# Seven products of quarters for every eight in the second mixture, with its weights streamed

## The chip, the core and the metric

The kernel runs on one core of one Trainium2 chip. The metric is the device time of one execution, in microseconds (us). Before the change it was 1636.01 us, the median of three runs (1632.27 to 1636.53). The execution that the profiler recorded took 1633.56 us.

TensorE (PE) multiplies matrices and writes the sums to eight banks of PSUM. VectorE (DVE) and ScalarE (ACT) read these banks and work on SBUF, GpSimd (POOL) works on SBUF alone, and SyncE (SP) issues most of the DMA transfers. Each of them takes its own instructions in order and waits at semaphores for the others.

## The reference

An attention without a softmax over scores gives 4608 tokens of 512 features. They go through a gated mixture, and then through a second one, which the change is about:

```python
def _moe_ref(x, w_gate, w_val, w_out, rms_g):
    rms = np.sqrt(np.mean(x * x, axis=-1, keepdims=True) + 1e-06)
    xn = x / rms * rms_g
    g = xn @ w_gate                      # 512 x 1536
    silu = g * (1.0 / (1.0 + np.exp(-g)))
    val = xn @ w_val                     # 512 x 1536
    return (silu * val @ w_out)          # 1536 x 512

def _moe2_ref(x, w1, w2, w3, w_out):
    h = np.maximum(np.maximum(x @ w1, x @ w2), x @ w3)   # each 512 x 768
    return (h @ w_out)                                   # 768 x 512
```

The weights arrive as 64-bit floats, which the kernel reads as pairs of 32-bit words and joins to 32-bit floats.

## The kernel before

The tokens are cut into nine groups of 512. Every matrix product is made of `128x512` matmuls in the type `fp32r`. As that type drops low bits, each operand is split into a high part `hi` (a cast, on ACT) and the rest `lo` (a subtraction, on DVE or POOL), and each block of a product takes three matmuls: hi by hi, hi by lo, lo by hi (`product_in`, L423; `three`, L430).

**The first mixture** fills the first two thirds of the time: 9 groups by 12 feature blocks `f`, in `iteration` (L494). One iteration has twelve matmuls for the gate into bank `G`, twelve for the value into bank `V`, and twelve of `out1` (L468) for the block before. Around them ACT takes the tanh of the gate (L541), DVE makes the product `t` and its `lo` part (L542, L553, L560), and the attention of the next group is computed in pieces. Three buffers with the tag `y` serve the squares of the norm (L329), the Newton steps, the results that leave for DRAM (L437) and the weights of the second mixture.

**The class `Ahead`** (L155) prepares those weights during groups 1 to 7, one step in each iteration: join the words of a piece of `128x512` into a `y` buffer (ACT, three instructions on DVE); split it into the piece's own load buffer `st` (ACT, POOL); write both parts to DRAM from `st` and load the next piece. There are 24 pieces: six feature blocks by three matrices, and six of the out matrix. In group 8, `fetch` (L196) brings everything back into SBUF, two transfers of 768 KB in each of eight iterations, to stay there.

**The second mixture** (L608) goes through the groups one by one, and through six feature blocks `f` in each: three products of twelve matmuls into the banks `G`, `V` and `a0`; a copy (L622) and two maxima (L624) that leave the largest in `t`; the split of `t` into `hh` and `hl`; and `out2` (L598), twelve matmuls for the block before. The inputs of the next group are loaded and split meanwhile (L480, L491).

The order of the instructions on each engine is set when the program is built, by a list scheduler that starts from the order of the code; a tile with a tag waits until its buffer is free. So the order that was written is kept on PE, while instructions of other engines and DMA issues move past each other.

Of the kernel before, what the change touches and what calls it, by code (L numbers as in the profile page):

```python
# [28 lines left out]

VW = 672  # L30
# [7 lines left out]
def attention_moe_moe(ctx: ExitStack, tc: tile.TileContext, q, k, kt, v, w1, rms_g, w2, w2_out, out):  # L38

# [42 lines left out]
    w2_dram = [dram.tile([P, 2, 3, N], F32, tag=f"w2_{s}", name=f"w2_dram_{s}") for s in range(NF2 + 2)]  # L82
# [72 lines left out]
    class Ahead:  # L155
# [4 lines left out]
        def __init__(self, pieces):  # L160
            self.pieces = pieces
            self.st, self.y = {}, {}
            self.loaded = 0

        def load(self):
            i = self.loaded
            if i < len(self.pieces):
                slot, j, src = self.pieces[i]
                self.st[i] = two.tile([P, 2 * N], I32, tag="st", name=f"st2_{slot}_{j}")
                nc.sync.dma_start(self.st[i], src.bitcast(I32))  # L170
# [272 lines left out]
    second = Ahead(  # L443
# [24 lines left out]
    def out1(g, f):  # L468
# [227 lines left out]
```

## Time and profile before

| what | us or share |
|---|---|
| median of three runs | 1636.01 |
| profiled execution, its own time | 1633.56 |
| its span, first to last instruction | 1631.8 |
| busy: PE, DVE, ACT, POOL | 97%, 45%, 30%, 12% |
| groups 1 to 7 of the first mixture, roughly 165 to 975 us | PE busy 809.68 of 810 |
| second mixture, from about 1038 us | PE busy without a gap to 1627.6 |

A matmul's row shows 0.39 us, but matmuls are pipelined, so what one costs is the distance between two starts. The granted clock of PE is 1.00 (the level of 2.4 GHz) from about 165 us to the end. Bytes: 130.15 MB in all, 80 GB/s on average.

### The profile page before, as it was taken

To read this page: it belongs to the slowest core of one execution; us is meant where nothing else is said; L and a number is where in the kernel's file an instruction comes from. 1 tells how busy PE (TensorE), PEld (TensorE's weight loads), DVE (VectorE), ACT (ScalarE), POOL (GpSimd) and SP (SyncE) were. 2 spreads that over 40 slices of the span, in tenths; PEclk is the share of its full clock that TensorE was granted. 3 is DMA by queue.
4 is the path that set the end of the run, shared out by engine and by line. 5 is a ranking of instruction groups with operands and counts; after the bars stand their busy time and mean duration, and the time that the engine had idled before them with its cause. 6 is when DMAs were issued, how large, how long until landed. Compare 5 with 4: busy or idle time off the path is not lost.

```text
span 1631.8 us, 18095 instructions
## 1 busy us (share of the span) xinstructions
PE 1585.3 (97%) x7190; PEld 1309.6 (80%) x7190; DVE 732.2 (45%) x1210; ACT 481.5 (30%) x806; POOL 199.4 (12%) x221
## 2 busy tenths in 40 slices
PE   5788999999999999999999999999999999999998
PEld 4576788888888888888888888888888888888887
DVE  6999655655646555565452422322222212222211
ACT  4554333433334333343332321211212112112111
POOL 4455121121221111212100000000000000000000
PEclk8899999999999999999999999999999999999999
DMA  7652241331423313313111045201101001010000
GB/s 257 255 191 79 92 132 58 116 96 48 138 88 111 113 58 117 107 55 111 55 46 33 6 162 194 78 0 52 52 1 52 26 27 52 1 52 26 1 26 26
DMA packets 72676, 130.15 MB, mean 80 GB/s; under 512 B 6032, under 2 KB 30608, under 8 KB 72592
## 3 DMA queue, kind: packets, MB, share of 16 engines
q1 hardware_dynamic: 62224, 110.12, 20.2%
q10 hardware_dynamic: 10368, 18.88, 3.2%
q8 instruction: 56, 0.92, 0.2%
q14 instruction: 28, 0.23, 0.0%
HBM read 95.42 MB, written 33.55 MB: 79 GB/s over the span
## 4 chain that ended last, share of the span: by engine, by line
PE 91%; DVE 5%; issue 2%; POOL 1%; DMA 1%; ACT 1%; SPq 0%; ACTq 0%; DVEq 0%; POOLq 0%
PE p L428 9%; PE p L427 9%; PE p L426 9%; PE acc L433 8%; PE acc L432 8%; PE acc L431 8%; PE pg L426 6%; PE pg L428 6%; PE pg L427 6%; PE pv L428 5%; PE pv L426 5%; PE pv L427 5%; PE pk L266 2%; DVE y L135 1%; PE pt L286 1%
## 5 line engine op out<-in xcount | busy, mean ns | idle before, releaser
L624 DVE TENSOR_TENSOR t<-t,p 128x512 f32<-128x512 f32 x108 | 74.2, 687 | 402.1 <-PE p L428 402.1
L542 DVE SCALAR_TENSOR_TENSOR t<-t,pg 128x512 f32<-128x512 f32 x106 | 72.7, 686 | 131.8 <-ACT t L541 130.8
L556 ACT CAST hh<-t 128x512 fp32r<-128x512 f32 x108 | 66.9, 619 | 159.4 <-DVE t L553 159.3
L541 ACT ACTIVATE t<-pg 128x512 f32<-128x512 f32 x106 | 63.1, 596 | 153.9 <-PE pg L428 153.9
L553 DVE TENSOR_TENSOR t<-t,pv 128x512 f32<-128x512 f32 x108 | 73.1, 677 | 59.6 <-PE pv L428 58.1
L560 DVE TENSOR_TENSOR hl<-t,hh 128x512 fp32r<-128x512 f32 x97 | 70.7, 729 | 60.5 <-ACT hh L556 59.8
L78 ACT CAST hh<-t 128x512 fp32r<-128x512 f32 x54 | 33.4, 618 | 210.2 <-DVE t L624 210.2
L622 ACT COPY t<-p 128x512 f32<-128x512 f32 x54 | 31.7, 587 | 192.7 <-PE p L428 192.7
L233 POOL TENSOR_TENSOR q<-q,qm 128x512 f32<-128x512 f32 x34 | 38.9, 1143 | 156.0 <-DVE qm L232 145.8
L190 POOL TENSOR_TENSOR st<-y,st 128x512 fp32r<-128x512 f32 x24 | 32.1, 1337 | 211.1 <-ACT st L189 190.2
L79 DVE TENSOR_TENSOR hl<-t,hh 128x512 fp32r<-128x512 f32 x54 | 37.4, 692 | 36.2 <-ACT hh L78 36.2
L242 POOL TENSOR_TENSOR q<-q,qr 128x512 f32<-128x512 f32 x34 | 38.6, 1137 | 61.0 <-DVE qr L241 59.0
L330 POOL TENSOR_TENSOR sacc<-sacc,sq 128x512 f32<-128x512 f32 x24 | 32.9, 1370 | 89.6 <-ACT sq L329 86.0
L266 PE MATMUL pk<-v,k 128*128 128x129 f32 x300 | 41.0, 286 | 1.1 <-DVE kv_raw L276 0.8
L432 PE MATMUL acc<-wl_(3, 1)_8004,hh 128*128 128x512 f32 x108 | 42.1, 389 | 0.0
L431 PE MATMUL acc<-wh_(3, 0)_7953,hh 128*128 128x512 f32 x108 | 42.0, 389 | 0.0
L432 PE MATMUL acc<-wl_(3, 0)_7954,hh 128*128 128x512 f32 x108 | 42.0, 389 | 0.0
L431 PE MATMUL acc<-wh_(3, 1)_8003,hh 128*128 128x512 f32 x108 | 42.0, 389 | 0.0
L433 PE MATMUL acc<-wh_(3, 0)_7953,hl 128*128 128x512 f32 x108 | 42.0, 389 | 0.0
L433 PE MATMUL acc<-wh_(3, 1)_8003,hl 128*128 128x512 f32 x108 | 42.0, 389 | 0.0
L266 PEld LDWEIGHTS pk<-v,k 128*128 128x128 f32 x300 | 37.9, 200 | 1.9 <-ACT qh L296 1.1
L438 ACT ACTIVATE oe<-acc 128x512 f32<-128x512 f32 x36 | 20.6, 597 | 50.2 <-PE acc L433 46.0
(474 smaller groups left out, 4438.9 us busy)
## 6 DMA issues: line engine op xcount, KB each, us to landing
words<-in_w SPq DMA_DIRECT2D x24, 768.0 KB, 7.2
w_dram<-st SPq DMA_DIRECT2D x24, 512.0 KB, 3.1
k<-in_k SPq DMA_DIRECT2D x30, 320.0 KB, 4.2
v<-in_v SPq DMA_DIRECT2D x30, 320.0 KB, 4.4
st<-in_w SPq DMA_DIRECT2D x18, 512.0 KB, 4.2
x<-xe ACTq DMA_DIRECT2D x36, 256.0 KB, 2.5
xraw<-x SPq DMA_DIRECT2D x36, 256.0 KB, 3.3
out<-oe ACTq DMA_DIRECT2D x36, 256.0 KB, 2.0
```

Of the source, the lines that this page charges most:

```text
L266: nc.tensor.matmul(pk[:, 0 : P + 1], k_t[g, p][:, c, :], v_t[g, p][:, c, :], start=(c == 0), stop=(c == 4))
L426: nc.tensor.matmul(pt, hi[:, j, s], xhs[kk], start=(kk == 0), stop=False)
L427: nc.tensor.matmul(pt, hi[:, j, s], xls[kk], start=False, stop=False)
L428: nc.tensor.matmul(pt, lo[:, j, s], xhs[kk], start=False, stop=(kk == 3))
L431: nc.tensor.matmul(pt, ah, bh, start=first, stop=False)
L432: nc.tensor.matmul(pt, ah, bl, start=False, stop=False)
L433: nc.tensor.matmul(pt, al, bh, start=False, stop=last)
L542: nc.vector.scalar_tensor_tensor(t, t, 1.0, pg, op0=ALU.add, op1=ALU.mult)
L553: nc.vector.tensor_mul(t, t, pv)
L556: nc.scalar.copy(hh[g, f], t)
L560: (nc.gpsimd if ahead else nc.vector).tensor_sub(hl[g, f], t, hh[g, f].bitcast(F32))
L624: nc.vector.tensor_max(t, t, pj)
```

## The change

The scheme is Strassen's, in Winograd's form, on 2 by 2 quarters. A *unit* `u` is one of the three matrices for a pair of feature blocks, `fp` and `fp + 3`; its left matrix has quarters of 128 features by 256 inputs, and its right one quarters of 256 inputs by 512 tokens, the tokens of two groups side by side. Instead of eight products of quarters (six matmuls each) there are seven. Four sums of the weights (`S1` to `S4`) are made once, in the preparation; four sums of the inputs (`T1` to `T4`) once for each of the four pairs of groups (`combine`). The seven products of a unit go into four banks `a` to `d` (tags `G`, `V`, `a0`, `a1`), three of them on top of what an earlier product left there, and the sums of the results are made by ACT, DVE and POOL (`unit`, L751). The ninth group is computed with four products of each unit, as before in amount.

Seven quarters of each of nine units, each hi and lo, make 63 pieces, kept in DRAM as 21 chunks of 768 KB; a ring of six buffers (`RING`) brings them in again for every pair, 84 chunks, and twelve more for the ninth group, these in three transfers each. The inputs take 28 planes in the buffers of the first mixture's weights. A step of `Ahead` now has a cost, and an iteration room for two or three of them (`advance`); a quarter that is written to DRAM sits in a `y` buffer until the write has landed. `out2` takes two feature blocks at a time, and at the end of a pair four calls stand together.

```diff
+UNITS = 9
+QUARTERS = 7
+CHUNK = 3
+A11, S2, S1, S3, A12, S4, A22 = range(QUARTERS)
+RING = ("wh0", "wl0", "wh1", "wl1", "wh2", "wl2")
+LATER_H = ("xh0", "xh1", "xh2", "xh3", "xl0", "xl1", "xl2", "xl3", "qh", "ql", "sacc", "kT")
...
-    w2_dram = [dram.tile([P, 2, 3, N], F32, tag=f"w2_{s}", name=f"w2_dram_{s}") for s in range(NF2 + 2)]
+    chunk_dram = [
+        dram.tile([P, CHUNK, 2, N // 2], F32, tag=f"w2_{c}", name=f"w2_dram_{c}")
+        for c in range(UNITS * QUARTERS // CHUNK)
+    ]
+    wo_dram = [dram.tile([P, 2, 3, N], F32, tag=f"wo_{s}", name=f"wo_dram_{s}") for s in range(2)]
...
+            self.steps = []
+            for u in range(UNITS):
+                self.steps += [(self.join, (2 * u,)), (self.join, (2 * u + 1,)), (self.sums, (u,))]
+                self.steps += [(self.quarter, (u, n)) for n in (A11, A12, S3, S4)] + [(self.load, ())]
+                self.steps += [(self.quarter, (u, n)) for n in (A22, S1, S2)] + [(self.load, ())]
+            for i in range(len(self.outs)):
+                self.steps.append((self.join, (2 * UNITS + i,)))
+                self.steps += [(self.half, (i, h)) for h in range(2)] + [(self.load, ())]
...
-        def step(self, n):
-            i, part = divmod(n, 3)
-            if i >= len(self.pieces):
-                return
-            slot, j, _ = self.pieces[i]
-            if part == 0:
-                words = self.st[i].rearrange("p (n t) -> p n t", t=2)
-                low, high = words[:, :, 0], words[:, :, 1]
-                nc.scalar.activation(high.bitcast(F32), high.bitcast(F32), AF.Copy, scale=2.0**-112)
-                self.y[i] = two.tile([P, N], F32, tag="y", name=f"y2_{i}", bufs=3)
-                y = self.y[i].bitcast(I32)
-                nc.vector.tensor_scalar(y, high, 3, None, op0=ALU.logical_shift_left)
-                nc.vector.scalar_tensor_tensor(y, high, -(2**31), y, op0=ALU.bitwise_and, op1=ALU.bitwise_or)
-                nc.vector.scalar_tensor_tensor(y, low, 29, y, op0=ALU.logical_shift_right, op1=ALU.bitwise_or)
-            elif part == 1:
-                st, y = self.st[i].bitcast(F32R), self.y.pop(i)
-                nc.scalar.copy(st[:, 0:N], y)
-                nc.gpsimd.tensor_sub(st[:, N : 2 * N], y, st[:, 0:N].bitcast(F32))
-            else:
-                st = self.st.pop(i).bitcast(F32).rearrange("p (t n) -> p t n", t=2)
-                nc.sync.dma_start(w2_dram[slot][:, :, j, :], st)
-                self.load()
...
+        def sums(self, u):
+            t = self.places(u)
+            nc.vector.tensor_add(t[S1], t["A21"], t[A22])
+            nc.vector.tensor_sub(t[S2], t[S1], t[A11])
+            nc.vector.tensor_sub(t[S4], t[A12], t[S2])
+            nc.vector.tensor_sub(t[S3], t[A11], t["A21"])
+
+        def split(self, src, dst, name):
+            t = two.tile([P, 2, N // 2], F32R, tag="y", name=name, bufs=3)
+            nc.scalar.copy(t[:, 0, :], src)
+            nc.gpsimd.tensor_sub(t[:, 1, :], src, t[:, 0, :].bitcast(F32))
+            nc.sync.dma_start(dst, t.bitcast(F32))
+
+        def quarter(self, u, n):
+            i = QUARTERS * u + n
+            self.split(self.places(u)[n], chunk_dram[i // CHUNK][:, i % CHUNK], f"wq_{u}_{n}")
...
+            room = 3 if 1 <= f <= 8 else 2
+            while self.steps:
+                step, args = self.steps[0]
+                writes = step in (self.quarter, self.half)
+                cost = 0 if step == self.load else 1 if writes else 2
+                if cost > room or writes and f > 9:
+                    return
+                room -= cost
+                self.steps.pop(0)
+                step(*args)
...
+    ring, fetched = {}, [0]
+    wanted = [(p, c, None) for p in range(NPAIR) for c in range(UNITS * QUARTERS // CHUNK)]
+    single = [QUARTERS * u + n for u in range(UNITS) for n in (A11, A12, S1, A22)]
+    wanted += [(NPAIR, c, single[CHUNK * c : CHUNK * c + CHUNK]) for c in range(len(single) // CHUNK)]
+
+    def fetch(count=1):
+        for _ in range(count):
+            i = fetched[0]
+            if i >= len(wanted):
+                return
+            p, c, parts = wanted[i]
+            t = wpool.tile([P, CHUNK, 2, N // 2], F32R, tag=RING[i % len(RING)], name=f"chunk_{p}_{c}")
+            if parts is None:
+                nc.sync.dma_start(t.bitcast(F32), chunk_dram[c])
+            else:
+                for n, part in enumerate(parts):
+                    nc.sync.dma_start(t[:, n].bitcast(F32), chunk_dram[part // CHUNK][:, part % CHUNK])
+            ring[p, c] = t
+            fetched[0] += 1
...
-            second.step(NF1 * (g - 1) + f)
-        if nxt is None and 1 <= f <= NF2 + 2:
-            second.fetch(f - 1)
+            second.advance(f)
+            if g == NG - 2 and f == NF1 - 1:
+                assert not second.steps
+        if nxt is None:
+            if 1 <= f <= 3:
+                fetch(2)
+            if f in (4, 5):
+                for n in range(4 * f - 16, 4 * f - 12):
+                    combine(0, n)
+            if f >= 6:
+                for which in {6: (B11,), 7: (T2,), 8: (T1,), 9: (T3,), 10: (B21, B22), 11: (T4,)}[f]:
+                    split_operand(which)
+            if f == 11:
+                fetch_out(0)
...
-    for g in range(NG):
-        for f in range(NF2):
-            if g + 1 < NG:
-                if f == 0:
-                    second_x(g + 1)
-                if 1 <= f <= 4:
-                    split_second_x(g + 1, f - 1)
-            wkey = (2, f)
-            banks = []
-            for j, tag in enumerate(("G", "V", "a0")):
-                pj = bank(tag, f"p2_{g}_{f}_{j}")
-                product_in(pj, wh[wkey], wl[wkey], j, xh2[g], xl2[g])
-                if j == 0:
-                    t = two.tile([P, N], F32, tag="t", name=f"t2_{g}_{f}")
-                    nc.scalar.copy(t, pj)
-                else:
-                    nc.vector.tensor_max(t, t, pj)
-            hh[g, f] = two.tile([P, N], F32R, tag="hh", name=f"hh2_{g}_{f}")
-            hl[g, f] = two.tile([P, N], F32R, tag="hl", name=f"hl2_{g}_{f}")
-            split(hh[g, f], hl[g, f], t)
...
+    def product2(pt, pr, n, which, first, last):
+        w = ring[pr, n // CHUNK][:, n % CHUNK]
+        for kk in range(2):
+            s = slice(kk * P, (kk + 1) * P)
+            i = 4 * which + 2 * kk
+            opens, ends = first and kk == 0, last and kk == 1
+            three(pt, w[:, 0, s], w[:, 1, s], plane(i), plane(i + 1), opens, ends, not first and pr < NPAIR)
...
+        def largest(dst, x, pt, y):
+            if j == 0:
+                nc.vector.tensor_add(dst, x, pt)
             else:
+                nc.vector.tensor_add(y, x, pt)
+                nc.vector.tensor_max(dst, dst, y)
+
+        product2(a, pr, n + A11, B11, True, True)
+        nc.scalar.copy(s1, a)
+        product2(b, pr, n + S2, T2, True, True)
+        nc.vector.tensor_add(u2, s1, b)
+        product2(c, pr, n + S1, T1, True, True)
+        nc.scalar.copy(s5, c)
+        nc.gpsimd.tensor_add(w, u2, s5)
+        product2(d, pr, n + S3, T3, True, True)
+        largest(t[1, 1], w, d, y0)
+        product2(a, pr, n + A12, B21, False, True)
+        if j == 0:
+            nc.scalar.copy(t[0, 0], a)
+        else:
+            nc.vector.tensor_max(t[0, 0], t[0, 0], a)
+        product2(c, pr, n + S4, B22, False, True)
+        largest(t[0, 1], u2, c, y1)
+        product2(d, pr, n + A22, T4, False, True)
+        largest(t[1, 0], u2, d, y0)
...
+            unit(pr, u, t)
+            consumed(pr, QUARTERS * (u + 1))
+            if j == 2:
+                for row in range(2):
+                    split_h(g, fp + H * row, t[row, 0], False)
+                for row in range(2):
+                    split_h(g + 1, fp + H * row, t[row, 1], True)
+            if pr == 0 and u == 0:
                 out1(NG - 1, NF1 - 1)
-    out2(NG - 1, NF2 - 1)
+                fetch_out(1)
+            if j == 0 and fp > 0:
+                out2(g, ACC, (fp - 1, fp - 1 + H))
+            if u == 1:
+                load_raw(pr + 1)
+            if 3 <= u < 7:
+                for n in range(2 * u - 6, 2 * u - 4) if pr + 1 < NPAIR else range(2) if u == 3 else ():
+                    combine(pr + 1, n)
+        for which in range(7) if pr + 1 < NPAIR else (B11, B21, T1):
+            split_operand(which)
+        out2(g + 1, ("G", "V", "a0", "a1"), (0, H, 1, 1 + H))
+        out2(g, ACC, (2, 2 + H), True)
+        out2(g + 1, None, (2, 2 + H), True)
...
```

**The second mixture on DVE**, where PE's banks are read. Before, one row of two maxima and a subtraction for each feature block (`p2` is the product in PSUM, `t2` the largest so far, `hl2` the low part):

```order
L624 TENSOR_TENSOR t2_0_1_8261<-t2_0_1_8261,p2_0_1_1_8263 128x512
L624 TENSOR_TENSOR t2_0_1_8261<-t2_0_1_8261,p2_0_1_2_8277 128x512
L79 TENSOR_TENSOR hl2_0_1_8292<-t2_0_1_8261,hh2_0_1_8291 128x512
L624 TENSOR_TENSOR t2_0_2_8326<-t2_0_2_8326,p2_0_2_1_8328 128x512
L624 TENSOR_TENSOR t2_0_2_8326<-t2_0_2_8326,p2_0_2_2_8342 128x512
L79 TENSOR_TENSOR hl2_0_2_8357<-t2_0_2_8326,hh2_0_2_8356 128x512
```

Now, the last unit of the first pair (`temps_wh9` holds s1, s5 and u2, `temps_wl9` holds w, y0 and y1; the rows on `x2_` are low parts of the next pair's inputs, from `sums_` and `raw2_`):

```order
L90 TENSOR_TENSOR x2_wl4_8175<-raw2_1_1_8599,x2_wh4_8172 128x512
L772 TENSOR_TENSOR temps_wh9_8452<-temps_wh9_8452,p2_0_8_V_9074 128x512
L90 TENSOR_TENSOR x2_wl4_8175<-sums_b_8071,x2_wl4_8175 128x512
L90 TENSOR_TENSOR x2_wh5_8226<-sums_b_8071,x2_wh5_8226 128x512
L90 TENSOR_TENSOR x2_wl5_8275<-sums_a_8070,x2_wh5_8226 128x512
L766 TENSOR_TENSOR temps_wl9_8453<-temps_wl9_8453,p2_0_8_a1_9076 128x512
L90 TENSOR_TENSOR x2_wl5_8275<-sums_a_8070,x2_wl5_8275 128x512
L767 TENSOR_TENSOR t2_0_2_t_8927<-t2_0_2_t_8927,temps_wl9_8453 128x512
L782 TENSOR_TENSOR t2_0_2_q_8924<-t2_0_2_q_8924,p2_0_8_G_9073 128x512
```

Eight instructions of a unit read the banks and the sums, and in a pair's last unit the subtractions for the next pair's inputs stand between them, ahead of the reads of bank `d` (tag `a1`, L766) and of bank `a` (tag `G`, L782).

**The first mixture on ACT**, between two tanh (L541 before, L651 now) of group 4. Before (`st2` and `y2` belong to `Ahead`):

```order
L541 ACTIVATE t_4_1_4221<-pg_4_1_4208 128x512
L189 CAST st2_4_0_3907<-y2_12_4194 128x512
L189 CAST st2_4_1_4107<-y2_13_4416 128x512
L556 CAST hh_4_1_4238<-t_4_1_4221 128x512
L78 CAST qh_5_0_4265<-pt_5_0_4260 128x512
L78 CAST kvh_5_0_4281<-kv_raw0_99 128x128
L541 ACTIVATE t_4_2_4315<-pg_4_2_4302 128x512
```

Now (`wq` is a quarter's `y` buffer, `st2_12` the next load):

```order
L651 ACTIVATE t_4_1_4351<-pg_4_1_4338 128x512
L226 CAST wq_5_3_4388<-st2_10_3803 128x256
L226 CAST wq_5_5_4392<-st2_10_3803 128x256
L666 CAST hh_4_1_4368<-t_4_1_4351 128x512
L226 CAST wq_5_6_4398<-st2_11_3895 128x256
L226 CAST wq_5_2_4490<-st2_11_3895 128x256
L89 CAST qh_5_0_4407<-pt_5_0_4402 128x512
L226 CAST wq_5_1_4494<-st2_11_3895 128x256
L204 ACTIVATE st2_12_4396<-st2_12_4396 128x512
L89 CAST kvh_5_0_4423<-kv_raw0_114 128x128
L651 ACTIVATE t_4_2_4457<-pg_4_2_4444 128x512
```

Five quarters are cast between the two tanh, out of three `y` buffers, and the scaling of the next load stands ahead of the second tanh too.

**SP's queue at the end of the first pair of the second mixture**. Before, SP had only the next groups' inputs (`xraw2`) to load there:

```order
L202 DMA wl_(3, 1)_8004<-w2_dram_7_85 128x1536
L489 DMA xraw2_1_0_8167<-x2_1_70 128x512
L489 DMA xraw2_1_1_8169<-x2_1_70 128x512
L489 DMA xraw2_1_2_8171<-x2_1_70 128x512
L489 DMA xraw2_1_3_8173<-x2_1_70 128x512
```

Now (`chunk_1_4` is chunk 4 for the second pair, `raw2_2` are the inputs of the third):

```order
L539 DMA chunk_1_3_9130<-w2_dram_3_81 128x1536
L572 DMA raw2_2_0_9427<-x2_4_73 128x512
L572 DMA raw2_2_1_9429<-x2_4_73 128x512
L539 DMA chunk_1_4_9132<-w2_dram_4_82 128x1536
L539 DMA chunk_1_5_9134<-w2_dram_5_83 128x1536
L575 DMA raw2_2_4_9435<-x2_5_74 128x1024
L572 DMA raw2_2_2_9431<-x2_4_73 128x512
L572 DMA raw2_2_3_9433<-x2_4_73 128x512
L575 DMA raw2_2_5_9437<-x2_5_74 128x1024
L539 DMA chunk_1_6_9362<-w2_dram_6_84 128x1536
```

The chunks 4 to 6 of the second pair stand behind loads of inputs, whose buffers come free when the second pair's inputs are split.

## Rows read from the trace of the kernel before

**Rows 1.** The page: span, busy shares, slices of PE and its clock.

```profile
span 1631.8 us, 18095 instructions
PE 1585.3 (97%) x7190; PEld 1309.6 (80%) x7190; DVE 732.2 (45%) x1210; ACT 481.5 (30%) x806; POOL 199.4 (12%) x221
PE   5788999999999999999999999999999999999998
PEclk8899999999999999999999999999999999999999
```

**Rows 2.** Windows by stage: length, engines' busy us, granted clock, DMA share, GB/s.

```profile
core 0: us, PE busy (x) PEld busy (x) DVE busy (x) ACT busy (x) POOL busy (x), PEclk, DMA share, GB/s
165.00:975.00 810.00, 809.68 (x3784) 675.01 (x3785) 434.98 (x769) 285.85 (x488) 122.13 (x144) 1.00 0.26 87
975.00:1038.00 63.00, 63.00 (x279) 52.17 (x279) 19.37 (x29) 12.75 (x22) 0.00 (x0) 1.00 0.45 156
1038.00:1168.00 130.00, 130.00 (x575) 107.64 (x575) 30.96 (x47) 24.19 (x43) 0.00 (x0) 1.00 0.10 35
```

**Rows 3.** Waits of PE from 165 us on: total us, times, longest.

```profile
PE pg L426 <- DVE t L542: 2.2, 1, 2.2
```

**Rows 4.** PE in order of time: start and length in us.

```profile
988.19 0.39 PE L426 MATMUL pg<-xh,wh_(1, 6)_902 128*128 128x512 f32 x1
...
996.35 0.39 PE L426 MATMUL pg<-xh,wh_(1, 7)_993 128*128 128x512 f32 x1
...
1045.31 0.39 PE L431 MATMUL acc<-hh,wh_(1, 11)_1311 128*128 128x512 f32 x1
...
1048.03 0.39 PE L426 MATMUL p<-x2h,wh_(2, 1)_7703 128*128 128x512 f32 x1
```

**Rows 5.** SP's issues in order of time, group 8.

```profile
988.16 0.32 SPq L201 DMA_DIRECT2D wh_(2, 4)_7853<-w_dram  x1
...
996.32 0.32 SPq L201 DMA_DIRECT2D wh_(2, 5)_7903<-w_dram  x1
```

**Rows 6.** DMA issues by line: count, KB each, median us from issue to landing.

```profile
w_dram<-st SPq DMA_DIRECT2D x24, 512.0 KB, 3.1
st<-in_w SPq DMA_DIRECT2D x18, 512.0 KB, 4.2
x<-xe ACTq DMA_DIRECT2D x36, 256.0 KB, 2.5
...
wh_(2, 3)_7803<-w_dram SPq DMA_DIRECT2D x1, 768.0 KB, 4.3
wl_(2, 3)_7804<-w_dram SPq DMA_DIRECT2D x1, 768.0 KB, 5.7
```

**Rows 7.** Groups by line: count, busy us, mean ns of one, idle before.

```profile
L624 DVE TENSOR_TENSOR t<-t,p 128x512 f32<-128x512 f32 x108 | 74.2, 687 | 402.1 <-PE p L428 402.1
L79 DVE TENSOR_TENSOR hl<-t,hh 128x512 fp32r<-128x512 f32 x54 | 37.4, 692 | 36.2 <-ACT hh L78 36.2
L78 ACT CAST hh<-t 128x512 fp32r<-128x512 f32 x54 | 33.4, 618 | 210.2 <-DVE t L624 210.2
L330 POOL TENSOR_TENSOR sacc<-sacc,sq 128x512 f32<-128x512 f32 x24 | 32.9, 1370 | 89.6 <-ACT sq L329 86.0
L190 POOL TENSOR_TENSOR st<-y,st 128x512 fp32r<-128x512 f32 x24 | 32.1, 1337 | 211.1 <-ACT st L189 190.2
L622 ACT COPY t<-p 128x512 f32<-128x512 f32 x54 | 31.7, 587 | 192.7 <-PE p L428 192.7
```

**Rows 8.** DVE and POOL in order of time, group 0.

```profile
99.79 0.96 DVE L153 TENSOR_TENSOR wl_(1, 5)_842<-y,wh_(1, 5)_820 128x768 fp32r<-128x768 f32 x1
...
132.72 2.16 POOL L153 TENSOR_TENSOR wl_(1, 8)_1097<-y,wh_(1, 8)_1075 128x768 fp32r<-128x768 f32 x1
133.10 2.59 DVE L153 TENSOR_TENSOR wl_(1, 8)_1097<-y,wh_(1, 8)_1075 128x768 fp32r<-128x768 f32 x1
```

**Rows 9.** Waits of SP's queue: total us, times, longest.

```profile
SPq L213 <- PE pt L286: 153.4, 17, 32.7
```

More of the change, by code (lines that the diff above doesn't have):

```diff
@@ L442, in attention_moe_moe @@
     first = Weights()
-    second = Ahead(
-        [(t, j, w2[t, :, j, :]) for t in range(NF2) for j in range(3)]
-        + [(NF2 + t, j, w2_out[t, :, j, :]) for t in range(2) for j in range(3)]
-    )
+    second = Ahead()
     for p in range(4):
@@ new lines, in place, with load_raw @@
+    def place(name, tag):
+        if name not in kept:
+            kept[name] = wpool.tile([P, 3, N], F32, tag=tag, name=name)
+        return kept[name]
+    B11, T2, T1, T3, B21, B22, T4 = range(7)
+    raw2 = {}
+    def load_raw(pr):
+        for kk in range(4):
+            raw2[0, kk] = one.tile([P, N], F32, tag=f"xraw{kk}", name=f"raw2_{pr}_{kk}")
+            nc.sync.dma_start(raw2[0, kk], x2_dram[2 * pr][:, kk, :])
+        for i in range(2 if pr < NPAIR else 0):
+            t = two.tile([P, 2, N], F32, tag="st", name=f"raw2_{pr}_{4 + i}")
+            nc.sync.dma_start(t, x2_dram[2 * pr + 1][:, 2 * i : 2 * i + 2, :])
+            raw2[1, 2 * i], raw2[1, 2 * i + 1] = t[:, 0, :], t[:, 1, :]
@@ L592, in attention_moe_moe, with evacuate2 @@
             iteration(g, nxt, f)
-        if nxt is None:
-            for kk in range(4):
-                split_second_x(0, kk)
-    def out2(g, f):
-        if f == 0:
-            acc[g] = [bank(f"acc{m}", f"acc2_{g}_{m}") for m in range(4)]
-        rh, rl = wh[3, f // 3][:, f % 3, :], wl[3, f // 3][:, f % 3, :]
+    def evacuate2(pt, g, m):
+        pool, tag, bufs = (one, "sacc", 1) if g == NG - 1 and m == 3 else (two, "y", 3)
+        e = pool.tile([P, N], F32, tag=tag, name=f"oe_{g}_{m}", bufs=bufs)
+        nc.scalar.copy(e, pt)
+        nc.scalar.dma_start(out[g * N + m * P : g * N + (m + 1) * P, :], e)
@@ L602, in out2 @@
+    acc2 = {}
+    def out2(g, tags, fs, last=False):
+        if g not in acc2:
+            acc2[g] = [bank(tag, f"acc2_{g}_{m}") for m, tag in enumerate(tags)]
+            begin = True
+        else:
+            begin = False
         for m in range(4):
             s = slice(m * P, (m + 1) * P)
-            three(acc[g][m], hh[g, f][:, s], hl[g, f][:, s], rh, rl, f == 0, f == NF2 - 1)
-            if f == NF2 - 1:
-                evacuate(acc[g][m], out[g * N + m * P : g * N + (m + 1) * P, :], f"oe_{g}", m, 1.0)
@@ new lines, in split_h, with consumed @@
+    def split_h(g, f, t, later):
+        for d, n, tag in ((hh, 2 * f, "hh"), (hl, 2 * f + 1, "hl")):
+            pool, tag = (one, LATER_H[n]) if later else (two, tag)
+            d[g, f] = pool.tile([P, N], F32R, tag=tag, name=f"{'hl'[n % 2]}2_{g}_{f}")
+        split(hh[g, f], hl[g, f], t)
+    ACC = tuple(f"acc{m}" for m in range(4))
+    H = NF2 // 2
+    done = [0]
+    def consumed(pr, n):
+        while done[0] < len(wanted) and (wanted[done[0]][0], CHUNK * wanted[done[0]][1] + CHUNK) <= (pr, n):
+            done[0] += 1
+            fetch()
@@ new lines, in attention_moe_moe @@
+    g = NG - 1
+    for u in range(UNITS):
+        fp, j = divmod(u, 3)
+        pair = [bank(tag, f"p2_{g}_{u}_{tag}") for tag in (("G", "V"), ("a0", "a1"))[u % 2]]
+        if j == 0:
+            t = [two.tile([P, N], F32, tag=tag, name=f"t2_{g}_{fp}_{tag}") for tag in ("q", "k")]
+        for row, (x, y) in enumerate(((B11, B21), (B11, T1))):
+            n = 4 * u + 2 * row
+            product2(pair[row], NPAIR, n, x, True, False)
+            product2(pair[row], NPAIR, n + 1, y, False, True)
+            if j == 0:
+                nc.scalar.copy(t[row], pair[row])
+            else:
+                nc.vector.tensor_max(t[row], t[row], pair[row])
+            if j == 2:
+                split_h(g, fp + H * row, t[row], True)
+        consumed(NPAIR, 4 * (u + 1))
+        if u == 3:
+            out2(g, ACC, (0, H))
@@ L637 @@
+    out2(g, None, (1, 1 + H))
+    out2(g, None, (2, 2 + H), True)
 def kernel(**inputs):
```

135 lines of the change are left out of this document (98 added, 37 removed).

## The prediction

> **What bounds the kernel now.** I read the page first: PE is busy in 97% of the span, the other engines in less than half of it, and the clock stands at its upper level from the third slice on [rows 1]. A busy PE row proves little, so I cut the span into stages. From 165 us to the end of the first mixture PE has no gap worth a word, nor has it one in the second [rows 2], and PE's list of waits has a single one after 165 us, of 2.2 us [rows 3]. The start, where PE does wait, is not touched by the change. Last I read PE in order of time, for what one matmul costs: from 988.19 to 996.35 us lie the 36 matmuls of one iteration, 8.16 us; from 1045.31 to 1048.03 us twelve of `out1`, which change the bank at every third, 2.72 us [rows 4]. Both give 0.2267 us for each, with or without a change of bank. So the time is the number of matmuls times 0.2267 us, from 165 us on, and an added wait costs only where PE has nothing else in front.
>
> **What the change removes.** Two groups cost 2 x 6 x 3 x 12 = 432 matmuls in the three products; now a unit has 7 x 6 = 42, and nine units 378. That is 54 fewer for each of the four pairs, 216 in all. The ninth group stays at 9 x 4 x 6 = 216, and the out products at 144 for a pair. 216 x 0.2267 us = 49.0 us. All of it lies on the path, as PE is never idle there.
>
> **What it adds on PE's path.** Units follow each other without a gap only if each bank has been read when PE comes back to it. A product takes 6 x 0.2267 = 1.36 us, a unit 9.52 us, and a result can be read 0.16 us after the last start's interval (0.39 less 0.2267, rows 4). The longest chain goes from the third product to the seventh, which writes onto bank `d` after the maximum of t[1,1] has read it: the third ends at 4.24 us in the unit; ACT's copy s5, 0.587 us (the copy of L622); POOL's sum w, 1.37 us (L330 is the same operation and size); DVE's addition, 0.687 us [rows 7]. With some 0.05 us at each of three handovers that is 7.0 us. PE needs the bank at 6 x 1.36 = 8.16 us: 1.1 us to spare. Banks `a` and `c` are read by one copy of 0.587 us and have at least two products of time. DVE has eight instructions in such a unit, 8 x 0.69 = 5.5 us of 9.52; with its share of splits and sums (12 + 8 + 14 for a pair, 24 us over 118 us) it is about two thirds busy. So inside a pair I cost the waits at nothing.
>
> In a pair's last unit it is tighter. There the scheduler put five subtractions for the next inputs around u2 and ahead of the reads of `d` and `a`. Counting 0.69 us each [rows 7]: two of them, then u2, end at about 4.3 us, three more at 6.4 us; w runs from 5.5 to 6.9 us; the addition that frees `d` ends at 7.65 us, in time; another subtraction, a maximum and the maximum that frees `a` end at 9.75 us, while the out products want bank `G` at 9.52 us. That is 0.25 us for each of four pairs, 1.0 us.
>
> DVE and POOL disturb each other, though: a subtraction of 768 columns takes DVE 0.96 us, but 2.59 us when it starts at 133.10 us beside POOL's, which runs until 134.88 us; the end, 135.69 us, is 0.81 us after POOL's [rows 8]. Where w and a subtraction meet, one of them is late by up to 0.7 us, twice in such a unit: 4 x (0.4 + 0.7) = 4.4 us instead of 1.0. The Trainium skill has this as a rule (SBUF — State Buffer, section "SBUF: two separate sides"): GpSimd and a VectorE instruction with two SBUF inputs take a shared pair of ports as an exclusive lock, and the later one stands still until the other is done. The rows at 133 us agree with it. If the ports were shared evenly instead, the sum would be the 1.0 us. I take 3 us, nearer to the row, and keep 0 and 5 us as ends.
>
> **The weights.** They were loaded once and stay; now a chunk of 768 KB is wanted for every 18 matmuls, 4.08 us, in the units, and none in the out products, 21.8 us at the end of a pair. The trace has this very rate: in group 8 SP issues two transfers of 768 KB every 8.16 us [rows 5], they land 4.3 and 5.7 us after their issue [rows 6], and PE's spacing in the same stretch is the 0.2267 us above [rows 4], at 156 GB/s over the stage [rows 2]. A ring of six is asked for some 20 us ahead. The inputs' loads that stand before chunks 4 to 6 of the next pair wait for splits that DVE finishes some 14 us after the last unit, and chunk 4 is wanted 21.8 + 16.3 us after it. Cost: nothing; if the cover went, a chunk that comes later than every 4.08 us costs its excess.
>
> **The preparation, in groups 1 to 6.** The joins keep their number, 24 with three DVE instructions each. The sums add 36 DVE instructions of 256 columns, at most 0.69 us each [rows 7], 25 us over some 600 us. ACT casts 75 pieces of 256 columns for 24 of 512, POOL subtracts as often: between half and all of 0.618 and 1.337 us each [rows 7], so +8 to +32 us and +18 to +68 us, on engines that are busy for 286 and 122 of 810 us [rows 2]; I take the halves. Work beside a full PE costs nothing by itself. What is new is that a `y` buffer is held until its write has landed: cast 0.31, POOL 0.67, landing 2.5 to 3.1 us (256 and 512 KB, rows 6), with the issue some 4.3 us. Between the two tanh of group 4 ACT has five casts for three buffers, then the scaling of a load that takes 4.2 us: the fourth cast waits for the first write, the scaling for the load behind the second one, and by these durations the second tanh is 0.5 us late. Late by how much does PE feel? Bank `G` is wanted again 24 matmuls after its product, 5.44 us, and tanh (taken as long as ACT's copy) and product take 0.59 + 0.69: 4.1 us to spare. I take 1.5 us for all places together, with ends at -1 us (the joins no longer take `y`) and 10 us.
>
> **The sum.** 1633.56 - 49.0 + 3 + 1.5 = 1589.1 us against the profiled execution, which lies 2.45 us under the median of the runs. A median of runs would be up to 1591.5; I say 1590 us, with 1583 (nothing lost) to 1600 us (both ends) as this case's own range.
>
> **Rivals.**
> 1. *The y buffers cost PE time.* If writes land as late as the second load of a couple (5.7 us) or wait in SP's queue behind loads, the tanh at about one place for each of the nine units and the six out pieces is late by 5 us and more. A stall of 1 us at fifteen places makes 1605 us. For it: three buffers for four users. Against: 4.1 us of slack each time.
> 2. *The chain through POOL sets the unit's length.* With a POOL sum of 1.37 us that first stands behind a DVE subtraction, and DVE's addition behind another, 7.0 + 1.4 = 8.4 us, 0.25 us too late; the eight units after a split are the candidates, and with other delays all 36: 36 x 0.5 us more makes 1608 us. Against: in most units DVE has nothing to do while w runs.
> 3. *Slower: the writes get stuck in SP's queue.* SP waits for buffers of `q` 17 times, 9.0 us on average and up to 32.7 us [rows 9]. Before, a write behind such a load held only its own load buffer; now it holds a `y` buffer, then ACT, then the tanh. With 17 such places at 9.0 - 4.1 us that is 83 us: 1673 us. It decides from 49 / 17 = 2.9 us a place on, a hold of 7 us beyond the normal. Against: the scheduler places a write after such a load only where it expects the load's buffer to be free by then, and both follow PE's pace.
> 4. *The ring runs dry.* If a chunk came every 6.2 us instead of 4.08, a pair would take 21 x 6.2 = 130 us, what its two groups take now, and the gain were gone. The transfers of rows 5 and 6 would have to be half as fast as they are.
>
> **Chances.** The forecast 0.74, rival 1 0.12, rival 2 0.08, rival 3 0.04, rival 4 0.02. Rivals 1 and 2 still are faster than before, rival 4 would leave the time where it was, and rival 3 is slower: faster by over 0.3% (5 us, about what runs that lie 4.3 us apart can tell) 0.94, within it 0.02, slower 0.04. The range 1582 to 1607 us takes in the forecast's own and the most of rivals 1 and 2.
>
> **What would show it.** Right: 216 fewer rows of 0.2267 us spacing, PE busy without gaps in the units, starts of equal units 9.52 us apart; a pause of 0.3 to 1 us before the first out product at the end of a pair; the first mixture ending where it did, near 1038 us. Wrong: PE waits named after L764 to L767 (rival 2) or after `chunk` (rival 4); tanh rows that start more than 4 us after their product, and a first mixture that ends later than 1045 us (rivals 1 and 3).

## The result, and the profile after

The changed kernel takes 1587.62 us (median of four runs, 1587.04 to 1588.73) against 1635.12 us in the runs beside it: a ratio of 0.9712, 95% interval 0.9696 to 0.9729, so 47.5 us or 2.9% faster. The forecast was 1590 us. The changed kernel's profiled execution took 1587.12 us, where the sum of the forecast had 1589.1 us.

The windows of the changed kernel, by the stages of [rows 2]:

```profile
core 0: us, PE busy (x) PEld busy (x) DVE busy (x) ACT busy (x) POOL busy (x), PEclk, DMA share, GB/s
165.00:975.00 810.00, 808.49 (x3778) 673.61 (x3779) 439.65 (x806) 296.63 (x538) 146.31 (x195) 1.00 0.30 96
975.00:1038.00 63.00, 63.00 (x280) 52.18 (x279) 34.70 (x54) 17.55 (x30) 0.00 (x0) 1.00 0.16 57
1038.00:1168.00 130.00, 130.00 (x573) 107.37 (x572) 62.93 (x97) 35.84 (x62) 12.94 (x10) 1.00 0.57 198
```

PE is as full as it was. In the second mixture DVE does twice the work and the DMA engines move 198 GB/s for 35, and neither is seen in PE's column. PE's list of waits from 165 us to the end (total, times, longest) says the same; its first line answers to [rows 3], and both waits lie before 185 us:

```profile
PE pg L475 <- DVE t L652: 2.2, 1, 2.2
PE rstd L435 <- DVE z L426: 0.4, 1, 0.4
```

The first matmuls of two units that follow each other (start, length), then the chain of the second unit through ACT, POOL and DVE, and the first matmul of its last product:

```profile
1169.59 0.39 PE L481 MATMUL p_G<-x_wh,chunk 128*128 128x512 f32 x1
...
1179.11 0.39 PE L481 MATMUL p_G<-x_wh,chunk 128*128 128x512 f32 x1
...
1183.45 0.59 ACT L774 COPY temps_wh<-p_a 128x512 f32<-128x512 f32 x1 [2.19 <-PE p_a L483]
...
1184.11 1.29 POOL L775 TENSOR_TENSOR temps_wl<-temps_wh 128x512 f32<-128x512 f32 x1 [8.23 <-ACT temps_wh L774]
...
1185.43 0.69 DVE L766 TENSOR_TENSOR temps_wl<-temps_wl,p_a 128x512 f32<-128x512 f32 x1 [2.64 <-POOL temps_wl L775]
...
1187.27 0.39 PE L481 MATMUL p_a<-x_wh,chunk 128*128 128x512 f32 x1
```

The units lie 9.52 us apart, 42 x 0.2267. The addition that frees bank `d` ends 7.01 us after the unit's start, the last product starts at 8.16: 1.15 us to spare, as worked out.

**A ruler.** From the first matmul of the second mixture to its last, the trace gives a length that no noise of the start touches. These are the two rows of the kernel before, and the two of the changed one:

```profile
1037.15 0.39 PE L426 MATMUL p<-x2h,wh_(2, 0)_7653 128*128 128x512 f32 x1
...
1627.16 0.39 PE L433 MATMUL acc<-wh_(3, 1)_8003,hl 128*128 128x512 f32 x1
```

```profile
1038.63 0.39 PE L481 MATMUL p_G<-x_wh,chunk 128*128 128x512 f32 x1
...
1581.44 0.40 PE L483 MATMUL acc<-wo_hi,l 128*128 128x512 f32 x1
```

590.01 us became 542.81, 47.20 less. The removed matmuls are 216 x 0.2267 = 48.97, so 1.77 us came back. The place is the out products: at a pair's end 96 of them run from 1137.91 to 1160.07 us, 22.16 us instead of 21.76, and 48 at the very end take 0.2 us too long. It is no wait, but a slower stream, 0.23 to 0.24 us from start to start:

```profile
1140.23 0.40 PE L482 MATMUL acc<-wo_lo,h 128*128 128x512 f32 x1
1140.47 0.40 PE L483 MATMUL acc<-wo_hi,l 128*128 128x512 f32 x1
1140.70 0.40 PE L481 MATMUL acc<-wo_hi,h 128*128 128x512 f32 x1
```

Outside the ruler the start gave 1.48 us more in this execution (1037.15 to 1038.63) and the tail, from the last matmul's start to the end of the span, 0.72 less (3.90 us instead of 4.62). 1633.56 - 48.97 + 1.77 + 1.48 - 0.72 = 1587.12 us: the whole difference is accounted for.

### The profile page after: what moved, and what is told of

It reads as the page before. It is cut to its first block, busy times and chain, and to the rows that moved or that the text cites. A ratio compares the mean times of both kernels' runs of the same rounds, so it can differ in the third digit from the quotient of the medians.

```text
span 1585.3 us, 18644 instructions
## 1 busy us (share of the span) xinstructions
PE 1538.8 (97%) x6974; PEld 1269.1 (80%) x6974; DVE 865.9 (55%) x1450; ACT 529.3 (33%) x919; POOL 270.1 (17%) x308
## 4 chain that ended last, share of the span: by engine, by line
PE 90%; DVE 5%; DMA 1%; issue 1%; POOL 1%; ACT 0%; SPq 0%; DVEq 0%; POOLq 0%; ACTq 0%
PE acc L482 9%; PE acc L481 9%; PE acc L483 9%; PE pg L475 6%; PE pg L477 6%; PE pg L476 6%; PE pv L477 6%; PE pv L476 6%; PE pv L475 6%; PE p_a L481 5%; PE p_a L483 5%; PE p_a L482 5%; PE p_G L481 2%; PE p_G L483 2%; PE p_G L482 2%; PE pk L315 2%
## 5 line engine op out<-in xcount | busy, mean ns | idle before, releaser
L775 POOL TENSOR_TENSOR temps_wl<-temps_wh 128x512 f32<-128x512 f32 x36 | 46.5, 1292 | 525.8 <-ACT temps_wh L774 517.5
L651 ACT ACTIVATE t<-pg 128x512 f32<-128x512 f32 x106 | 62.9, 594 | 126.4 <-PE pg L477 126.3
L483 PE MATMUL p_a<-x_wh,chunk 128*128 128x512 f32 x240 | 93.4, 389 | 0.0
L481 PE MATMUL p_a<-x_wh,chunk 128*128 128x512 f32 x240 | 93.4, 389 | 0.0
L482 PE MATMUL p_a<-x_wl,chunk 128*128 128x512 f32 x236 | 91.8, 389 | 0.0
L482 PE MATMUL acc<-wo_lo,h 128*128 128x512 f32 x216 | 84.8, 392 | 0.0
L481 PE MATMUL acc<-wo_hi,h 128*128 128x512 f32 x216 | 84.6, 392 | 0.0
L483 PE MATMUL acc<-wo_hi,l 128*128 128x512 f32 x216 | 84.4, 391 | 0.0
L227 POOL TENSOR_TENSOR wq<-st,wq 128x256 fp32r<-128x256 f32 x63 | 47.5, 770 | 166.2 <-ACT wq L226 160.3
L483 PEld LDWEIGHTS p_a<-x_wh,chunk 128*128 128x128 f32 x240 | 45.1, 188 | 9.4
L481 PEld LDWEIGHTS p_a<-x_wh,chunk 128*128 128x128 f32 x240 | 45.0, 188 | 9.3
L482 PEld LDWEIGHTS p_a<-x_wl,chunk 128*128 128x128 f32 x236 | 44.3, 188 | 9.2
L481 PE MATMUL p_G<-x_wh,chunk 128*128 128x512 f32 x123 | 47.8, 389 | 0.0
```

The costliest lines, as they stand in the source:

```text
L227: nc.gpsimd.tensor_sub(t[:, 1, :], src, t[:, 0, :].bitcast(F32))
L481: nc.tensor.matmul(pt, ah, bh, start=first, stop=False, skip_group_check=onto)
L482: nc.tensor.matmul(pt, ah, bl, start=False, stop=False, skip_group_check=onto)
L483: nc.tensor.matmul(pt, al, bh, start=False, stop=last, skip_group_check=onto)
L651: nc.scalar.activation(t, pg, AF.Tanh, scale=0.5)
```

## The experiments

**The start, first.** The kernel before was run once more, unchanged, for its own scatter.

> The kernel before once more, for a second profile of its start. In its first profile the second mixture starts at about 1037.2 us, in the changed kernel's at 1038.6 us, and in the ten variants of the changed kernel between 1037.5 and 1040.9 us; the first mixture's steady part takes the same time in both. Theory (the start varies from run to run, whatever the kernel): the second mixture starts at another time here, 1038 to 1040 us, with a time of 1634.5 to 1636.5 us. Rival (the change makes the start 1 to 2 us longer): again near 1037.2 us, and a time near 1633.5 us.

1636.7 us. Its second mixture starts 3.1 us later than in the first profile and is 590.01 us long again:

```profile
1040.26 0.39 PE L426 MATMUL p<-x2h,wh_(2, 0)_7653 128*128 128x512 f32 x1
...
1630.27 0.39 PE L433 MATMUL acc<-wh_(3, 1)_8003,hl 128*128 128x512 f32 x1
```

So the start varies by 3 us whatever the kernel, and most of the 1.48 us of the changed kernel's profile need not be the change's doing. A part of it is, though. PE's wait for `z`, the second line of its list above, stands in the profiles of the changed kernel and all its variants (0.2 to 1.8 us), and in neither profile of the kernel before. There `z`, the result of the Newton steps for group 1, was ready 6.7 us before PE wanted it:

```profile
168.19 0.16 DVE L377 SCALAR_TENSOR_TENSOR z<-a,z 128x4 f32<-128x4 f32 x1
...
175.08 0.60 PE L386 MATMUL rstd<-ident,z 128*128 128x128 f32 x4
```

In the changed kernel DVE has joins and sums of `Ahead` between the Newton steps (one of the sums is the first row), and PE waits for the last step:

```profile
174.62 0.43 DVE L221 TENSOR_TENSOR st<-st,st 128x256 f32<-128x256 f32 x1
...
176.21 0.16 DVE L426 SCALAR_TENSOR_TENSOR z<-a,z 128x4 f32<-128x4 f32 x1
...
176.52 0.62 PE L435 MATMUL rstd<-ident,z 128*128 128x128 f32 x4 [0.41 <-DVE z L426]
```

Below, small effects are read from the ruler.

**Eight products again, all else kept.**

```
         product2(d, pr, n + A22, T4, False, True)
+        product2(d, pr, n + A22, T4, False, True)
```

> In every unit of the four pairs the last product is issued a second time onto the same bank: eight products as before the change, everything else of the change kept (in this run t[1,0] holds that product twice). Theory (the time is the count of matmuls, and weights from DRAM, sums and waits are hidden): 216 x 0.2267 = +49.0 us, 1587.6 + 49.0 = 1636.6 us, equal units 10.88 us apart, pairs 118.7 + 12.2 = 130.9 us. Against the kernel before (1635.1 us) that leaves 1.5 us for all that the change adds. Rival (the units lose time in waits, which an added product would fill): under +45 us, below 1633 us.

1636.92 us, ratio to before 1.0015 (1.0005 to 1.0025); the ruler 591.69 us, 48.88 more than the changed kernel's. The gain is PE's work and nothing else, and all that the change adds, streaming and sums and quarters, costs 0.15% by the ratio, or 1.68 us by the ruler against the kernel before.

**How much room the chain has.** POOL's sum `w` made twice, then three times:

```
         nc.gpsimd.tensor_add(w, u2, s5)
+        nc.gpsimd.tensor_add(w, u2, s5)
```

> POOL makes the sum w of every unit twice, with the same result. In the trace of the changed kernel DVE's addition behind w ends 7.01 us after the unit's start and PE wants bank d at 8.16 us. Theory (1.15 us to spare): one sum more, 1.29 us, ends the addition at 8.30 us; PE waits 0.15 to 0.25 us in each of 36 units, +5 to +9 us, 1593 to 1597 us. Rival a (the chain through POOL is nowhere near the bound): no change, 1587.6 us. Rival b (the chain already sets the unit): +1.29 us in each unit, +46 us, 1634 us.

> The sum w three times, with the same result. Theory: the addition ends at 7.01 + 2.58 = 9.59 us, 1.43 us after PE wants the bank; with the handover 1.45 to 1.55 us in each of 36 units, +52 to +56 us, 1640 to 1644 us, and the second extra sum costs 46 us where the first cost 5 to 9. Rival a (chain nowhere near): 1587.6 us. Rival b (chain sets the unit): +93 us, 1680 us.

1611.99 us (ratio to before 0.9859, 0.9845 to 0.9874) and 1658.57 us (1.0147, 1.0132 to 1.0162); rulers 567.18 and 613.09 us. The second extra sum costs 45.9 us, 1.28 for each of 36 units: past the edge the chain sets the time. The edge is where it was read from the rows, but the first extra sum cost 24.4 us instead of 5 to 9. One plain unit with the doubled sum shows the first part of that (DVE, weight load and matmul in order of time):

```profile
1184.89 0.69 DVE L766 TENSOR_TENSOR temps_wl<-temps_wl,p_a 128x512 f32<-128x512 f32 x1 [4.03 <-POOL temps_wl L776]
...
1185.63 0.19 PEld L481 LDWEIGHTS p_a<-x_wh,chunk 128*128 128x128 f32 x1 [0.54 <-DVE temps_wl L766]
1185.63 0.50 PE L481 MATMUL p_a<-x_wh,chunk 128*128 128x512 f32 x1
...
1185.97 0.39 PE L482 MATMUL p_a<-x_wh,chunk 128*128 128x512 f32 x1
```

The product starts 8.45 us into its unit instead of 8.16: 0.29, for two sums and the gap between them. Then the first matmul after the wait takes 0.34 us to the next start instead of 0.23; its weights are loaded only then (the row of PEld), not beneath an earlier matmul. With that the unit is 9.95 us long, 0.43 more. The rest is uneven: a unit that follows a split and has out products behind it lengthens by 1.0 us, and the step over a pair's end by 1.9 (0.8 at the last pair). In the former DVE's subtractions, pushed back by the late addition before them, stand ahead of `u2`, and POOL starts 5.56 us into the unit instead of 5.00 (at 1202.65 us in the unit from 1197.09 on). PE's list names both places, though it sees only 9.1 us of the 24.4:

```profile
PE p_a L481 <- DVE t_t L764: 5.2, 8, 0.7
PE p_a L481 <- DVE temps_wl L766: 3.9, 4, 1.1
```

**The sum on DVE.**

```
-        nc.gpsimd.tensor_add(w, u2, s5)
+        nc.vector.tensor_add(w, u2, s5)
```

> The sum w made by DVE instead of POOL; POOL then has nothing to do in the second mixture. Theory (chain and pair's end have slack): no change in time, 1586.5 to 1588.7 us; DVE's subtraction beside w in a pair's last unit, 1.79 us in the changed kernel, is 0.69 us; the addition behind w ends near 6.4 us instead of 7.01 us in a unit. Rival (POOL's share of the chain costs PE time in the units or at the pair's end): 0.3 us or more in each of 36 units less, below 1577 us.

1588.97 us, ratio 0.9717 (0.9703 to 0.9731); ruler 542.73 us. No change, so POOL's link costs nothing. What the lock does is seen at a pair's end. The changed kernel, DVE and POOL:

```profile
1132.90 0.69 DVE L90 TENSOR_TENSOR x_wh<-sums_b,x_wh 128x512 fp32r<-128x512 f32 x1
1133.50 1.79 DVE L90 TENSOR_TENSOR x_wl<-sums_a,x_wh 128x512 fp32r<-128x512 f32 x1
1135.21 0.67 DVE L766 TENSOR_TENSOR temps_wl<-temps_wl,p_a 128x512 f32<-128x512 f32 x1
...
1137.02 0.67 DVE L782 TENSOR_TENSOR t_q<-t_q,p_G 128x512 f32<-128x512 f32 x1
1137.61 0.68 DVE L90 TENSOR_TENSOR x_wh<-raw,x_wh 128x512 fp32r<-128x512 f32 x1
```

```profile
1133.39 1.35 POOL L775 TENSOR_TENSOR temps_wl<-temps_wh 128x512 f32<-128x512 f32 x1 [8.23 <-ACT temps_wh L774]
```

With the sum on DVE, the same place:

```profile
1134.27 0.69 DVE L775 TENSOR_TENSOR temps_wl<-temps_wh 128x512 f32<-128x512 f32 x1
1134.88 0.69 DVE L90 TENSOR_TENSOR x_wl<-sums_a,x_wh 128x512 fp32r<-128x512 f32 x1
```

The subtraction took 1.79 us beside POOL and 0.69 without: 1.1 us, once in such a unit (0.7 at the end of the fourth pair). That agrees with the lock of [rows 8]. It agrees, too, with the Trainium skill's rule that the prediction quotes (SBUF — State Buffer, section "SBUF: two separate sides"): the subtraction ends 0.55 us after POOL's sum.

**The pair's end without DVE's subtractions.**

```
-            split(plane(n), plane(n + 1), operand(which, kk))
+            nc.scalar.copy(plane(n), operand(which, kk))      # from the second pair on
...
-            three(..., plane(i), plane(i + 1), ...)
+            three(..., plane(i), plane(i + (pr == 0)), ...)
```

> From the second pair on the low parts of the inputs are not made (the high part stands in their place; PE's work is the same), so DVE has 14 subtractions fewer at the end of each of the first three pairs and 6 fewer at the end of the fourth. In the changed kernel no PE wait is seen there, but the 96 out products at a pair's end take 22.13 to 22.16 us where 96 x 0.2267 makes 21.76. Theory a (PE's stream is slowed by DVE's and ACT's work beside it): 21.76 us in each of the four, 1.5 us off the time. Theory b (it lies in the out products themselves): 22.13 us stays, and the time. In both no wait appears or goes: 1586 to 1588.5 us. If the forecast's term of 3 us for the pair's end had been real, it would go here: 1584.6 us.

1588.47 us, ratio 0.9714 (0.9698 to 0.973); ruler 542.73 us, the 96 out products still 22.13 us. So there was no pair-end wait to win back. Beside these products DVE's work fell from 14.3 to 8.9 us and their time stayed, so it is not what slows them.

**In sixes.** At a pair's end two calls of 24 in place of one of 48:

```
-        out2(g + 1, ("G", "V", "a0", "a1"), (0, H, 1, 1 + H))
+        out2(g + 1, ("G", "V", "a0", "a1"), (0, H))
+        out2(g + 1, None, (1, 1 + H))
```

> At a pair's end the first 48 out products are issued in two calls of 24, six matmuls into a bank before the next bank instead of twelve; the same result. The out products inside a pair, in sixes, cost 0.2267 us each; these 48 cost 0.233. Theory a (the twelve in a row make the difference): 21.8 us instead of 22.13 to 22.16 at each pair's end, 1.3 us less in all, 1586.3 us. Theory b (it is something else in these products): no change, 22.1 us.

1587.03 us, ratio 0.9708 (0.9693 to 0.9722); 21.95 to 21.98 us at each end, the ruler 542.05 us. Half of the excess goes with the order, half stays. Neither theory is right, and why these products stream slower stays open.

**Two y buffers instead of three** (`bufs=2` at each tile with the tag).

> Two buffers with the tag y instead of three. In the changed kernel ACT waits 13 times for a y buffer's write, 20.3 us in all, 2.6 us at most, and no tanh starts more than 1.7 us after its gate product, of 4.1 us that were counted as slack. A write holds its buffer for some 5 us (cast 0.42, POOL 0.74, landing 3.4, handovers); with two buffers three quarters in an iteration make ACT wait some 4 us. Theory (4.1 us of slack at each gate): 0 to 8 us more, 1588 to 1596 us, with tanh rows up to 4 us and more behind their product. Rival (a y buffer's wait reaches PE directly): 25 iterations with three quarters at 2 to 4 us each, +50 to +100 us, 1638 to 1688 us.

1589.15 us, ratio 0.9721 (0.9707 to 0.9736); ruler 542.79 us, no PE wait after 180 us. ACT's waits for a write (total, times, longest), with three buffers and with two:

```profile
ACT wq L226 <- DMA w_dram<-wq: 20.3, 13, 2.6
```

```profile
ACT wq L226 <- DMA w_dram<-wq: 28.3, 20, 2.5
```

Even two do not reach PE; the latest tanh is then 2.9 us behind its product (472.65 us). The latest tanh of the changed kernel is 1.7 us behind its product (end of the matmul 323.09), and ahead of it stands the scaling of `k`, not a cast:

```profile
322.70 0.39 PE L477 MATMUL pg<-xh,wl_(1, 3)_675 128*128 128x512 f32 x1
```

```profile
324.18 0.74 ACT L306 ACTIVATE k<-k 128x640 f32<-128x640 f32 x1 [0.36 <-DVE k L305]
324.82 0.58 ACT L651 ACTIVATE t<-pg 128x512 f32<-128x512 f32 x1
```

**The ring, of three and of two.**

```
-    RING = ("wh0", "wl0", "wh1", "wl1", "wh2", "wl2")
+    RING = ("wh0", "wl0", "wh1")                  # then ("wh0", "wl0")
...
             three(pt, w[:, 0, s], w[:, 1, s], ...)
+        consumed(pr, n + 1)                           # asked for after each product
```

> Three buffers for the streamed weights instead of six, asked for again after each product instead of after each unit. A chunk is then asked for 8.16 us before it is wanted; it lands 4.0 to 5.0 us after its issue. Theory (what matters is that a chunk lands within the use of the other two, and the DMA engines are far from full): no change, 1586.5 to 1589 us, no PE wait for a chunk in the units. Rival (the transfers are near their limit, and the six buffers hide delays): waits named after the chunk, 0.5 us for each of 84, +40 us.

> Two buffers for the streamed weights: a chunk can be asked for only when the one before the last is used up, 4.08 us before it is wanted, and in the changed kernel it lands 4.0 to 5.0 us after its issue. Theory (the cover is that time and nothing else): 0.16 us to the end of the last matmul, 0.1 us at each of two handovers and 4.2 us of landing make a wait of 0.5 us, with 0.14 us for PE's start after a wait 0.6 us, for some 86 chunks: +52 us, 1640 us (between +35 and +110), and waits named after the chunk. Rival (a transfer alone on the engines lands faster than beside others): no or little change, below 1600 us.

Three: 1588.8 us, ratio 0.9719 (0.9704 to 0.9733), ruler 542.80 us, nothing lost. Two: 1616.41 us, ratio 0.9892 (0.9876 to 0.9909), ruler 567.99 us, so 25.2 us for some 86 chunks, 0.29 each on average where I had 0.6, and below the range that I gave; the waits have the name that rival 4 asked for:

```profile
PE p_a L481 <- DMA chunk<-w_dram: 10.2, 20, 3.3
PE p_G L481 <- DMA chunk<-w_dram: 3.0, 10, 0.4
PE p_V L481 <- DMA chunk<-w_dram: 0.9, 1, 0.9
```

The mechanism is right, landing against the time of one chunk, and the size half of what I took. Three buffers hold, two do not.

**The ninth group.** First only its matmuls cut to 256 columns:

```
-            product2(pair[row], NPAIR, n, x, True, False)
-            product2(pair[row], NPAIR, n + 1, y, False, True)
+            for c in (slice(0, N // 2), slice(N // 2, N)):
+                product2(pair[row][:, c], NPAIR, n, x, True, False, c)
+                product2(pair[row][:, c], NPAIR, n + 1, y, False, True, c)
```

> The ninth group's 216 matmuls of 512 columns become 432 of 256 columns, the same result. It asks whether the seven products could be had for a single group, with its two halves of tokens in place of two groups. Theory a (cost goes by columns): 0.1133 us each, no change, 1587.6 us; seven products on halves would then save 27 x 0.2267 = 6.1 us. Theory b (linear between 0.104 us of the rows of 128x129 and 0.2267 of 128x512, so 0.145 us each): +13.6 us, 1601 us, and seven products on halves would cost 5.8 us more than now.

1591.71 us, ratio 0.9733 (0.9719 to 0.9748); ruler 545.69 us, 2.88 more for 432 matmuls of 256. From start to start 0.120 us, between the two theories: 0.0067 us more than half of 0.2267, so seven products on halves save 3.6 us. (The 0.104 us in the second theory is misread: rows of 128x129 start 0.112 us apart in the steady part of the changed kernel, so that its line would give 0.150 us, further off still.) Then the seven products for the ninth group too, its two halves of 256 tokens in place of two groups:

```
-    wanted += [(NPAIR, c, single[CHUNK * c : CHUNK * c + CHUNK]) for c in range(len(single) // CHUNK)]
+    wanted = [(p, c, None) for p in range(NPAIR + 1) for c in range(UNITS * QUARTERS // CHUNK)]
...
+        if pr == NPAIR:
+            a, b, c, d, s1, s5, u2, w, y0, y1 = (x[:, L] for x in (a, b, c, d, *temps))
...
-            product2(pair[row], NPAIR, n, x, True, False)
-            product2(pair[row], NPAIR, n + 1, y, False, True)
+        unit(NPAIR, u, t)                             # t: column halves of two tiles
```

> The ninth group by the seven products too: its two halves of 256 tokens in place of two groups, 378 matmuls of 256 columns instead of 216 of 512, all 21 chunks of weights instead of 12. Theory (PE's work alone: a matmul of 256 columns costs 0.120 us): 378 x 0.120 = 45.4 us instead of 49.0, -3.6 us, 1584.0 us. Rival a (transfers): a chunk is wanted every 18 x 0.12 = 2.16 us, 364 GB/s; six lie ready, fifteen more come in some 50 us if one lands every 2.9 us (two in 5.7 us, rows 6), which is just in time; at one every 4.2 us they take 63 us and the time is about 10 us above 1587.6. Rival b (the chain through ACT, POOL and DVE, with halves 0.35 + 0.67 + 0.37 us and three handovers, sets the unit): it ends at 3.9 us of 4.32, so no.

1585.46 us (1584.07 to 1586.08), ratio 0.9697 (0.9682 to 0.9711): the fastest measured, though its interval overlaps the changed kernel's. The ruler decides: 539.22 us, 3.59 less, as worked out. The transfers kept up:

```profile
1517.00:1560.00 43.00, 43.00 (x334) 41.80 (x333) 19.73 (x48) 9.67 (x24) 5.17 (x7) 1.00 0.81 288
```

That is the window of the ninth group: 288 GB/s, DMA share 0.81, and PE without a gap.

## Why the prediction was right, step by step

- **The matmuls: right.** 216 fewer at 0.2267 us. With the eighth product put back the time came back (48.88 us on the ruler).
- **Waits inside a pair at nothing: right,** with the chain at 7.01 us where 7.0 was worked out. That it is so close is luck: POOL's sum took 1.29 us instead of 1.37, and the three handovers 0.20 instead of 0.15. What the forecast did not say is how dear the edge is: in the run with a second sum the product was late by 0.3 us in a plain unit, and the loss was 0.68 us a unit on average, because PE's restart adds 0.1 us and late additions push the subtractions and the next `u2` behind them.
- **The pair's end, 3 us: wrong, it is 0.** Before any lock, the forecast had the addition that frees `d` end 7.65 us into the last unit and the maximum that frees `a` at 9.75. The first pair's last unit starts at 1128.39 us, 9.52 before its first out product; there the two end at 7.49 and 9.30 us, with the lock in them. Two steps failed. The first is "Counting 0.69 us each". The length of a DVE row is not what one costs in a queue: its starts lie 0.60 us apart, and a row of the kernel before has it, three of them in 1.90 us, which is twice 0.60 and once 0.69:

```profile
1037.78 1.90 DVE L79 TENSOR_TENSOR x2l<-xraw,x2h 128x512 fp32r<-128x512 f32 x3 [1.08 <-ACT x2h L78]
```

  The Trainium skill (Perfetto Trace Analysis, section "Optimizing Scalar/DVE Operations") says that part of a profiled latency overlaps with the next instruction; these rows agree, with 0.09 us of 0.69. Behind the addition stand three instructions, so this takes off 0.3 us. The second is what the lock adds. The sum `w` ran from 5.00 to 6.35 us into the unit, not from the 5.5 to 6.9 for which the forecast shows no row. The subtraction that the lock held ended at 6.90; without the lock DVE would have stood waiting for `w` until 6.35 anyway. So the lock's 1.1 us moved the addition by some 0.45 us (an estimate from these rows), once in the unit, where the forecast took the two meetings to make the unit 0.4 + 0.7 us late; its 0.4 is worked out nowhere. The maximum that frees bank `G` ends at 1137.69 us and PE takes the bank at 1137.91, without a pause. I had read PE by distances and DVE by lengths.
- **The weights at nothing: right,** with half of the ring unused.
- **The `y` buffers, 1.5 us: wrong, they are 0,** and 0 with two buffers. The slack of 4.1 us was never used up, as the latest tanh is 1.7 us behind its product, and 2.9 with two buffers. The estimate should have followed it: a delay of 0.5 us behind 4.1 us of slack is nothing, not a part of 0.5.
- **Not foreseen:** 1.77 us in the out products, half of it by their order, the rest open; 0.72 us less at the tail; and at the start, which the forecast took as untouched by the change, the wait for `z`, 0.41 us, with joins and sums of the weights standing between the Newton steps on DVE. These and the start's scatter make 2.5 us and stand where the two wrong terms stood with 4.5, so the sum was closer than its terms. That is luck.
- **The rivals.** 1 fell with two buffers, 2 with the sum on DVE. 3: PE has no wait behind a tanh after 185 us, so no write was stuck long enough to matter. 4 is real, but only with a ring of two.

## What to carry to other kernels

Where PE has no gap, count its matmuls by the distance of their starts and ask of all else only whether it ends before PE comes back; take that from distances on the other engines too, not from row lengths. A margin is worth measuring by adding work to the chain: here the room read from the rows, 1.15 us, held, and the first step past it cost more than twice the overrun. For small effects measure between two rows inside the trace, since the start alone moved by 3 us.

## What the runs showed of the hardware

A matmul of 128x256 costs 0.120 us and one of 128x512 0.2267, so halving the columns costs 6%. After a wait the first matmul takes 0.34 us to the next start instead of 0.23. Weights streamed at 288 GB/s left PE's spacing as it was. Rows of DVE on 128x512 are 0.69 us long and start 0.60 us apart; one that met a sum of POOL took 1.79. The out products whose spacing grew to 0.23 to 0.24 us have no wait and a granted clock of 1.00, and are as slow with less work of DVE beside them; what slows them was not found.
